# Linear attention with a feed-forward block on one core: batch 0's values in two loads, the first denominators in two single banks, and a new order for both

## The chip, the cores and the metric

The kernel runs on one core of a Trainium2 chip. The metric is the device time of one execution in microseconds (us). TensorE multiplies matrices, VectorE and ScalarE do elementwise work and empty PSUM (the banks that TensorE writes), GpSimd does a few small operations, and SyncE issues every load and store. In the rows of the profile these are PE (PEld is its weight load), DVE, ACT, POOL and SP.

## The reference

```
q_p, k_p = phi(q), phi(k)            # 4 batches, 4 heads, 1088 positions, 32 -> 64 features
kv  = sum over s of k_p[s,f] * v[s,d]
z   = sum over s of k_p[s,f]
att = (q_p @ kv) / (q_p @ z + 1e-6)  # phi(x)[i*8+j] = (S1 x)[i] * (S2 x)[j]
x   = att with the heads side by side        # 4352 tokens x 128
h   = relu(x @ w_in)                         # 128 -> 2048
out = (s * h*h + b) @ w_out                  # 2048 -> 128
```

## The kernel before

The 4352 tokens are cut into nine tiles, the first of 256 tokens and eight of 512. For each batch the kernel forms the key features and sums them with the values; for each tile it forms the query features, numerators and denominators, divides, and runs the feed-forward block over eight pairs of hidden blocks. From tile 1 on, every feed-forward product is split into three passes on high and low parts; tile 0 is multiplied in one float32 form.

The work is written as generators, and one string, `ORDER`, is the whole program order: each token advances the generator of that name by one step, and a step's instructions go to their engines in that order. A second table, `ON_DVE`, lists the steps that go to VectorE instead of ScalarE or GpSimd. Every engine takes its instructions strictly in the order in which they were written.

The names that matter here:

- `c` and `z` are filler products of 256 and 512 columns on TensorE, written to a spare bank.
- `Ls`, `Lk0`, `Lv0`, `Lq1`, `Lw6` and the like issue loads on SyncE: the projections, keys, values, queries of tile 1, weights. `Lw2i` and `Lw2i+1` are block i of `w_in` and `w_out`, loaded in pieces of 256 KB; blocks 0 and 1 are one piece each, blocks 2 to 4 two pieces each. The tiles are `raw` in the rows. Below, "w6's second piece" is the second load of `Lw6`.
- `s` unpacks the projections into `sk` and copies them twice into `srep`; `w0`, `w1`, ... unpack weights (an activation on ScalarE, a shift of the low words on either engine, a join on VectorE).
- `k0`, `e0`, `v0` are the key features, key sums and value sums of batch 0. `k0` works in three groups of three chunks: projections in a bank `psa`, a copy to `kab`, and their outer product `ph`, which `v0` then sums with the values. `e0` and `v0` end in two copies into `st`.
- `q0`, `q1` are the query features of tiles 0 and 1 (two tiles `hp`, copies `br`, products `pq`). `q2` and later go a longer way: a small product into `hp` (line 419), a copy `abq`, a store to DRAM and loads back that spread it, the last four into `br`.
- `d0` and `n0` are the denominators and numerators of tile 0, `n1` both of tile 1. `00` to `07` are the feed-forward pairs of tile 0, `10` to `17` those of tile 1.

PSUM is in three pools: `hp` (two tiles of two banks), `ops` (one bank) and `psa` (three single banks).

SyncE has eight completion counters that its transfers take in turn, so a transfer is issued only when the one eight places earlier has landed. When SyncE issues one after such a wait thus tells when the earlier one landed.

The constants (own heads, identity, scale and bias) lie behind the values of batch 0 in one array and arrive in the same load, into `vc_sb`.

Of the kernel before, what the change touches and what calls it, by code (L numbers as in the profile page):

```python
# [9 lines left out]
F32 = mybir.dt.float32  # L10
# [28 lines left out]
DIRECT = (0, 1)  # L39
FIRST_F32 = (0, 1, 2, 3, 4, 5, 6, 7)  # L40
ORDER = """
c z Ls c z Lk0 c Lk0 Lw0 Lw2 s Lv0 Lq1 Lw8 z s c z c s s z z s w0 w2 k0 z s c k0 Lw6 k0 k0 k0 Lw1 k0 k0 w0 k0 w0 Lw4
Lw6 q0 c q0 Lq2 k0 Lw4 q0 Lw3 Lw5 Lw5 Lw7 Lw7 e0 e0 q0 Lw8 Lk1 e0 v0 v0 q0 w2 Lk1 e0 v0 w2 v0 q1 q1 q1 q1 e0 e0 w1
v0 z w1 q1 d0 v0 n1 d0 n0 w6 w6 q2 d0 c w4 d0 d0 n0 n1 Lv1 w4 w4 w1 q2 w4 w3 00 00 00 01 w3 w0 03 01 01 w5 w6 q2 00
02 Lw9 03 w8 w3 n1 w3 n1 01 03 Lw9 02 w5 04 02 w7 q2 w5 w7 n1 Lk3 q2 w0 03 05 n1 05 Lk3 02 w8 Lq3 w1 05 Lq4 q1 n1 04
q2 n1 k1 w8 06 w6 w7 04 n1 w9 05 07 06 w3 04 k1 w4 06 k1 n1 w9 w9 k1 w9 07 13 k1 07 w1 Lv1 Lv3 w6 06 q2 w5 13 13 10
q2 07 q2 k1 k3 10 q3 10 q3 13 14 10 07 w2 q2 13 k1 k3 k1 12 w2 w5 14 q3 k1 10 15 w7 q2 07 12 Lv2 14 12 k1 q3 Lk2 k3
10 k3 12 Lv3 11 14 w8 k3 12 w7 n2 k3 15 12 14 w8 07 q3 w9 15 n2 n2 13 14 11 15 11 17 n2 n2 Lk2 15 n2 16 15 q3 q3 n2
n2 11 11 Lq6 17 q4 q3 k2 16 n2 n2 20 k3 16 11 16 17 q3 q4 25 16 q4 17 q3 k3 q4 q4 16 20 22 20 k2 17 17 25 25 20 25
17 20 22 17 24 20 q4 22 q3 k2 22 25 24 24 k3 q4 Lv2 23 22 n3 q4 Lq5 23 24 q6 n3 23 q6 22 n3 Lq8 n3 24 21 23 21 27 q6  # L50
21 n3 k2 q4 25 23 q6 21 n3 27 26 24 n3 23 k2 27 n3 21 k2 q6 27 q8 q6 n3 q6 q6 n3 26 q4 26 k2 21 q0 30 q8 q4 k2 k2 27
q6 26 33 q6 k3 30 k2 30 q8 26 q5 n4 q5 q8 33 32 n4 30 30 26 33 n4 27 n4 n4 33 n4 33 32 31 q6 32 34 n4 27 31 30 31 32
31 n6 32 Lq7 n4 31 q5 n6 35 q8 q8 n6 34 32 q5 n6 31 34 n6 n6 35 34 n6 35 q5 36 37 n6 n6 35 q8 34 n6 34 36 61 33 36
35 37 36 35 60 37 37 36 27 61 63 q5 36 37 q8 q5 37 q8 61 61 60 60 64 61 37 63 63 60 60 q8 64 n4 63 63 64 65 60 q5 62
q8 64 65 61 64 62 65 q7 n8 n4 63 62 67 q7 n8 65 65 n8 62 q5 n8 62 q7 n8 66 67 q5 67 64 66 67 q7 65 67 66 q5 66 40 n8
42 66 40 n8 40 42 62 41 42 n5 66 40 q7 n5 n5 67 40 n8 42 41 45 67 n5 q7 44 41 42 n5 q7 40 n5 n5 41 45 43 45 41 45 45
42 43 n5 45 44 43 44 43 47 46 41 44 43 47 47 44 67 43 q7 46 46 n8 n5 n5 47 46 47 51 51 54 q7 n8 51 44 46 50 54 54 q7
51 51 46 47 54 50 54 53 50 47 56 53 52 50 53 q7 50 n7 50 52 54 n7 52 53 47 55 53 51 52 55 n7 52 55 85 53 56 55 55 56
57 57 57 52 56 56 n7 n7 55 85 57 80 57 81 85 56 85 57 80 85 81 n7 80 81 80 57 80 83 83 81 84 80 85 86 81 83 83 83 81
84 84 82 84 86 84 86 n7 84 n7 n7 86 n7 87 82 82 83 57 86 87 71 87 72 87 82 82 72 87 72 71 86 72 70 72 71 82 70 74 71  # L60
87 71 70 70 76 70 74 87 70 37 73 76 76 74 76 71 72 74 76 73 75 74 77 73 76 73 73 75 87 75 73 77 75 77 74 75 75 77 77
77 77 77 77 77 77
"""
ON_DVE = frozenset("""
a4 a6 a7 e1 e2 e3 e4 e5 e6 e7 e8 k0 m2 m3 m4 m5 m6 m7 m8 o00 o03 o06 o10 o15 o20 o25 o30 o35 q40 q43 q44 q50
q52 q76 q80 q81 r22 r24 r33 r37 r50 r61 r63 r65 r66 r76 r77 r87 s0 sb t1 t2 u13 u16 u20 u24 u26 u32 u33 u34
u36 u41 u44 u45 u47 u51 u55 u56 u57 u60 u62 u63 u65 u70 u71 u72 u73 u77 u81 u82 u83 u86 w0h w0l w1h w1l w2h
w2l w3b w3h w3l w4b w4h w4l w5b w5l w6l w7l w8b w8l w9b w9h w9l x2 x3 x4 x5 x8 y0 y3
""".split())
NS = 32 * 2 + 2 * R  # L70
CS, CB, CT = 0, 1, 32
# [28 lines left out]
def attn_ffn_kernel(ctx: ExitStack, tc: tile.TileContext, qT, kq, vc, s80, w_in, w_out, outT):  # L100
    nc = tc.nc
# [288 lines left out]
    qfeat, xhl, x_first = {}, {}, []  # L390
# [55 lines left out]
    def moving(pq, rows, h, e0, e1):  # L446

        if len(pq.shape) == 3:
            return [(pq[rows, h, e0:e1], e0, e1)]
        if (e0, e1) == (0, 2 * QUARTER):  # L450
            return [(pq[rows, h], e0, e1)]
        cuts = [e0, QUARTER, e1] if e0 < QUARTER < e1 else [e0, e1]
        return [(pq[rows, h, a // QUARTER, a % QUARTER:a % QUARTER + e - a], a, e) for a, e in zip(cuts, cuts[1:])]

    def parts_of(t, out, y, pq, start):
        halves = tiles[t][2]
        for k in range(max(len(x) for x in halves)):
            for h in range(H):
                for r in range(2):
                    if k < len(halves[r]):  # L460
                        b, e0, e1 = halves[r][k]
                        rows = slice(64 * r, 64 * r + 64)
                        for x, a, e in moving(pq, rows, h, e0, e1):
                            nc.tensor.matmul(out[r][32 * h:32 * h + 32, a:e], st_t[b][rows, y, h // 2, h % 2], x,  # L464
                                             start=(a == 0 and start), stop=True, skip_group_check=True)

    def inverse(dt, C, kept):
        rc = p1.tile([P, 32], F32, name="rc")
        nc.vector.tensor_scalar(out=rc[:, :2 * C], in0=dt.rearrange("p (c y) -> p c y", y=32)[:, :, 0],
                                scalar1=EPS, scalar2=None, op0=ALU.add)  # L470
# [261 lines left out]
```

## Time and profile before

| what | value |
|---|---|
| three timed runs | 228.83, 230.77, 230.79 us |
| their median | 230.77 us |
| the profiled execution | 229.11 us |
| its span, first to last instruction | 227.3 us |
| TensorE busy | 222.1 us |
| VectorE busy | 188.9 us |
| ScalarE busy | 176.6 us |
| loads and stores | 22.08 MB |

The profiled execution lasts 1.8 us longer than its span; that part lies around the instructions. Times in the rows further down are counted from the start of the span. Instructions of one engine overlap in their pipeline, so the start of the next one often lies before the end of the last.

### The profile page before, as it was taken

Reading aid. Unit: us, or ns where it says so; the run is one execution under the profiler, and the core shown is the slowest. Engines: PE = TensorE matmul, PEld = TensorE weight load, DVE = VectorE, ACT = ScalarE, POOL = GpSimd, SP = SyncE. Lnnn points to the kernel's source line nnn. Section 1 sums busy time; section 2 is a strip of 40 time slices with the busy share of each in tenths; the row PEclk is TensorE's granted clock in tenths of the full one; section 3 lists DMA queues with packets and bytes.
Section 4 is the critical chain, followed back from the end, with each engine's and each line's share of the span. In section 5 each row is a group of like instructions: output and inputs, shape, how many; then the busy total and the mean of one; then the engine's idle time right before and its main releaser. Section 6 shows DMA issues by size and latency. Waiting matters only on the chain.

```text
span 227.3 us, 4622 instructions
## 1 busy us (share of the span) xinstructions
PE 222.1 (98%) x1840; PEld 176.8 (78%) x1840; DVE 188.9 (83%) x269; ACT 176.6 (78%) x211; POOL 4.6 (2%) x14
## 2 busy tenths in 40 slices
PE   8989999999999999999999999999999999999994
PEld 5658788787877787888887878888878888887883
DVE  1979889998799969999778979997976597968682
ACT  3489989998968959886875779669767969788671
POOL 1001220000000000000000000000000000000000
PEclk9999999999999999999999999999999999999999
DMA  6999583830157443054000321200100001001001
GB/s 190 375 369 375 191 250 108 267 114 3 46 174 195 138 146 92 27 176 128 0 0 13 92 61 46 72 0 0 46 3 1 0 37 55 0 3 46 0 0 46
DMA packets 12204, 22.08 MB, mean 97 GB/s; under 512 B 1304, under 2 KB 2840, under 8 KB 12184
## 3 DMA queue, kind: packets, MB, share of 16 engines
q1 hardware_dynamic: 12184, 21.80, 29.3%
q8 instruction: 14, 0.23, 0.4%
q14 instruction: 6, 0.05, 0.1%
HBM read 18.65 MB, written 3.15 MB: 96 GB/s over the span
## 4 chain that ended last, share of the span: by engine, by line
PE 93%; DMA 3%; SPq 1%; ACT 1%; DVE 1%; issue 0%
PE hp L571 42%; PE ops L571 42%; PE psa L464 4%; DMA vc_sb<-vc 3%; PE psa L253 2%; PE hp L419 1%; PE psa L352 1%; PE hp L402 0%; SPq L185 0%; SPq L158 0%; PE hp L464 0%; ACT ot L619 0%; DVE pq L410 0%; PE psa L274 0%; ACT br L121 0%
## 5 line engine op out<-in xcount | busy, mean ns | idle before, releaser
L565 DVE TENSOR_TENSOR ul<-u,uh 128x1024 fp32r<-128x1024 f32 x64 | 77.8, 1218 | 8.4 <-ACT uh L121 6.3
L133 ACT ACTIVATE u<-hp 128x1024 f32<-128x1024 f32 (+1 forms) x60 | 57.8, 965 | 20.6 <-PE hp L571 9.7
L142 ACT ACTIVATE u<-u 128x1024 f32<-128x1024 f32 (+1 forms) x64 | 64.1, 1006 | 4.9 <-DVE u L131 3.5
L571 PE MATMUL hp<-xh,wil 128*128 128x512 f32 x128 | 51.1, 399 | 0.0
L571 PE MATMUL ops<-uh,wol 128*128 128x512 f32 (+1 forms) x128 | 50.4, 394 | 0.0
L571 PE MATMUL hp<-xl,wih 128*128 128x512 f32 x128 | 49.9, 390 | 0.0
L571 PE MATMUL hp<-xh,wih 128*128 128x512 f32 x128 | 49.9, 390 | 0.0
L571 PE MATMUL ops<-uh,woh 128*128 128x512 f32 (+1 forms) x128 | 49.6, 388 | 0.0
L121 ACT CAST uh<-u 128x1024 fp32r<-128x1024 f32 x34 | 35.6, 1052 | 7.0 <-DVE u L140 3.4
L571 PE MATMUL ops<-ul,woh 128*128 128x512 f32 (+1 forms) x128 | 39.3, 388 | 0.0
L121 DVE CAST uh<-u 128x1024 fp32r<-128x1024 f32 x30 | 20.7, 688 | 11.0 <-ACT u L142 10.6
L571 PEld LDWEIGHTS ops<-uh,wol 128*128 128x128 f32 x128 | 24.0, 188 | 6.8 <-issue 1.6
L571 PEld LDWEIGHTS hp<-xh,wil 128*128 128x128 f32 x128 | 24.0, 188 | 6.2 <-ACT u L133 0.5
L571 PEld LDWEIGHTS hp<-xl,wih 128*128 128x128 f32 x128 | 24.0, 188 | 5.2
L571 PEld LDWEIGHTS ops<-ul,woh 128*128 128x128 f32 x128 | 24.0, 188 | 5.1
L571 PEld LDWEIGHTS ops<-uh,woh 128*128 128x128 f32 x128 | 24.0, 188 | 4.7
L571 PEld LDWEIGHTS hp<-xh,wih 128*128 128x128 f32 x128 | 24.1, 188 | 4.7
L131 DVE TENSOR_SCALAR u<-hp 128x1024 f32<-128x1024 f32 x12 | 14.7, 1224 | 1.9 <-PE hp L571 1.0
L136 DVE TENSOR_TENSOR ph<-kab 128x768 f32<-128x768 f32 (+2 forms) x9 | 10.8, 1214 | 0.1
L464 PE MATMUL psa<-pq,st 64*32 64x256 f32 (+2 forms) x336 | 10.2, 330 | 0.0
L140 DVE TENSOR_TENSOR u<-u 128x1024 f32<-128x1024 f32 x8 | 9.6, 1215 | 0.4 <-ACT u L133 0.3
L202 ACT ACTIVATE w<-raw 128x512 f32<-128x512 f32 (+1 forms) x10 | 5.9, 587 | 4.3 <-DMA raw<-w_in 4.2
(86 smaller groups left out, 172.6 us busy)
## 6 DMA issues: line engine op xcount, KB each, us to landing
pq<-qd SPq DMA_DIRECT2D x14, 256.0 KB
br<-qd SPq DMA_DIRECT2D x28, 128.0 KB
raw<-w_in SPq DMA_DIRECT2D x8, 256.0 KB
qt<-qT SPq DMA_DIRECT2D x8, 256.0 KB
raw<-w_out SPq DMA_DIRECT2D x8, 256.0 KB
outT<-ot SPq DMA_DIRECT2D x7, 256.0 KB
kt<-kq SPq DMA_DIRECT2D x3, 320.0 KB
vt<-vc SPq DMA_DIRECT2D x3, 320.0 KB
```

The source lines that it names most:

```text
L121: (nc.vector.tensor_copy if key in ON_DVE else nc.scalar.copy)(out=out, in_=in_)
L131: nc.vector.tensor_scalar(out=out, in0=in_, scalar1=0.0, scalar2=None, op0=ALU.max)
L133: nc.scalar.activation(out=out, in_=in_, func=AF.Relu)
L136: (nc.vector if key in ON_DVE else nc.gpsimd).tensor_tensor(out=out, in0=in0, in1=in1, op=op)
L140: nc.vector.tensor_tensor(out=out, in0=in_, in1=in_, op=ALU.mult)
L142: nc.scalar.activation(out=out, in_=in_, func=AF.Square)
L202: nc.scalar.activation(out=out, in_=f32(high), func=AF.Prelu, scale=2.0 ** -112, alpha=2.0 ** 32)
L253: nc.tensor.matmul(out[32 * q:32 * q + 32], w, x, start=(q not in begun), stop=last, skip_group_check=True)
L352: nc.tensor.matmul(views[e][32 * q:32 * q + 32], sp[64 * e:64 * e + 64], kt[64 * e:64 * e + 64, a:a + w32], start=True, stop=True, skip_gr ...
L464: nc.tensor.matmul(out[r][32 * h:32 * h + 32, a:e], st_t[b][rows, y, h // 2, h % 2], x, start=(a == 0 and start), stop=True, skip_group_ch ...
L565: nc.vector.tensor_tensor(out=ul[:, :, :N], in0=u[:, :, :N], in1=f32(uh[:, :, :N]), op=ALU.subtract)
L571: nc.tensor.matmul(out, w, x, start=(first and k == 0), stop=(last and k == len(terms) - 1))
```

## The change

The load of `vc_sb` (662 KB) becomes two: values of chunks 0 to 5 (384 KB), then values of chunks 6 to 8 with the constants (278 KB). The first denominators no longer use an `hp` tile, but two `psa` banks, and are transposed by two instructions in place of one. `ORDER` and `ON_DVE` are written anew for both. From `44 43 ... q7 46 46 n8 n5 n5 47 46 47 51` to the end the order string is the same; ahead of that the feed-forward pairs keep nearly their sequence.

```
-VPARTS = [(VW + NCST,)] + [(5 * H * D, 4 * H * D)] * 3
+VPARTS = [(6 * H * D, 3 * H * D + NCST)] + [(5 * H * D, 4 * H * D)] * 3
...
     def first_denominators():
         M = TILES[0] // 2
-        den = ps_h.tile([P, 2, 512], F32, name="hp")
-        parts_of(0, [den[:, r, :M] for r in range(2)], 1, qfeat[0], True)
+        den = [ps_a.tile([P, 512], F32, name="psa")[:, :M] for r in range(2)]
+        parts_of(0, den, 1, qfeat[0], True)
         yield
         dt = p1.tile([P, NMAX], F32, name="dt")
-        nc.vector.transpose(out=dt[:, :2 * M].rearrange("p (r m) -> p r m", r=2), in_=den[:, :, :M])
+        for r in range(2):
+            nc.vector.transpose(out=dt[:, r * M:(r + 1) * M], in_=den[r])
         yield
         yield from inverse(dt[:, :2 * M], M // 32, first)
...
-c z Ls c z Lk0 c Lk0 Lw0 Lw2 s Lv0 Lq1 Lw8 z s c z c s s z z s w0 w2 k0 z s c k0 Lw6 k0 k0 k0 Lw1 k0 k0 w0 k0 w0 Lw4
+c z c Ls Lk0 Lk0 z Lw2 c c s s z c Lw0 w2 c c c s c z s k0 z c k0 Lv0 Lv0 w2 Lq1 s k0 c k0 c w0 w0 Lw1 k0 k0 w0 Lw6
...
-a4 a6 a7 e1 e2 e3 e4 e5 e6 e7 e8 k0 m2 m3 m4 m5 m6 m7 m8 o00 o03 o06 o10 o15 o20 o25 o30 o35 q40 q43 q44 q50
+a7 e1 e2 e3 e4 e5 e6 e7 e8 k0 k1 k2 m2 m3 m4 m5 m6 m7 m8 o00 o03 o06 o10 o15 o20 o25 o30 o35 q43 q50 q52 q64
...
```

On TensorE, from the end of the query features of tile 1 to the first feed-forward product (lines 277 and 274 end `e0` and `v0`, lines 650 and 651 are filler, 464 is `d0`, `n0` and `n1`, 419 is `q2`), before:

```order
L277 MATMUL psa<-vc_sb,zm 128x4
L274 MATMUL psa<-vc_sb,kvs 128x128
L650 LDWEIGHTS const-bfloat16-1.0
L650 MATMUL ops<-const-bfloat16-1.0 128x512
L464 MATMUL hp<-pq,st_291 32x128 x8
L464 MATMUL psa<-pq,st_291 32x256 x16
L464 MATMUL hp<-pq,st_291 32x128 x8
L419 MATMUL hp<-qt,sq 32x128 x8
L650 LDWEIGHTS const-bfloat16-1.0
L650 MATMUL ops<-const-bfloat16-1.0 128x256
L571 MATMUL hp<-x,w_00_92 128x256 x2
```

The same place after the change:

```order
L277 MATMUL psa<-vc_sb,zm 128x4
L274 MATMUL psa<-vc_sb,kvs 128x128
L651 LDWEIGHTS const-bfloat16-1.0
L651 MATMUL ops<-const-bfloat16-1.0 128x256
L651 LDWEIGHTS const-bfloat16-1.0
L651 MATMUL ops<-const-bfloat16-1.0 128x256
L464 MATMUL psa<-pq,st_302 32x128 x8
L464 MATMUL hp<-pq,st_302 32x128 x8
L419 MATMUL hp<-qt,sq 32x128 x8
L464 MATMUL psa<-pq,st_302 32x256 x16
L651 LDWEIGHTS const-bfloat16-1.0
L651 MATMUL ops<-const-bfloat16-1.0 128x256
```

`n0` has moved from behind `n1` to directly behind `d0`, and `q2` from behind `n1` to ahead of it.

On ScalarE, from the unpacked projections to the copies into `st` (lines 202 and 127 unpack weights; `w_10` is `w2`, `w_00` is `w0`, `w_01` is `w1`), before:

```order
L202 ACTIVATE sk<-s_raw 128x80
L121 COPY srep<-sk 128x64
L202 ACTIVATE w_00_92<-raw_114 128x256
L202 ACTIVATE w_10_94<-raw_116 128x256
L127 ACTIVATE raw_114<-raw_114 128x256
L121 COPY kab_137<-psa 128x2x96
L121 COPY br<-hp 128x2x128 x2
L127 ACTIVATE raw_116<-raw_116 128x256
L121 COPY br<-hp 128x512 x2
L121 COPY st_291<-psa 128x128
L202 ACTIVATE w_01_93<-raw_156 128x256
```

The same place after the change:

```order
L202 ACTIVATE w_10_94<-raw_113 128x256
L121 COPY srep<-sk 128x64
L127 ACTIVATE raw_113<-raw_113 128x256
L121 COPY srep<-sk 128x64
L202 ACTIVATE w_00_92<-raw_122 128x256
L127 ACTIVATE raw_122<-raw_122 128x256
L121 COPY kab_132<-psa 128x2x96
L121 COPY br<-hp 128x2x128 x2
L202 ACTIVATE w_01_93<-raw_156 128x256
L121 CAST wih<-w_00_92 128x256
L127 ACTIVATE raw_156<-raw_156 128x256
L121 COPY br<-hp 128x512 x2
```

Both copies into `srep` now stand on ScalarE behind the unpacking of `w2` (VectorE made one of them before), and the unpacking of `w1`, a cast and a shift stand ahead of the copies `br` of tile 1 instead of behind them.

On SyncE, the loads from the values of batch 0 to `w4`'s second piece (buffer numbers kept; 123 is `w8`, 148 `w6`, 156 `w1`, 166 `w4`, 121 and 191 the queries of tiles 1 and 2), before:

```order
L158 DMA vc_sb_82<-vc 128x1324
L176 DMA qt_121<-qT 128x512
L185 DMA raw0_123<-w_in 128x512
L185 DMA raw0_148<-w_in 128x512
L185 DMA raw1_156<-w_out 128x512
L185 DMA raw0_166<-w_in 128x512
L185 DMA raw0_148<-w_in 128x512
L176 DMA qt_191<-qT 128x512
L185 DMA raw0_166<-w_in 128x512
```

The same place after (156 is `w1`, 161 `w6`, 163 `w4`, 166 `w8`, 144 and 168 the queries):

```order
L158 DMA vc_sb_82<-vc 128x768
L158 DMA vc_sb_82<-vc 128x556
L176 DMA qt_144<-qT 128x512
L185 DMA raw1_156<-w_out 128x512
L185 DMA raw0_161<-w_in 128x512
L185 DMA raw0_163<-w_in 128x512
L185 DMA raw0_166<-w_in 128x512
L176 DMA qt_168<-qT 128x512
L185 DMA raw0_161<-w_in 128x512
L185 DMA raw0_163<-w_in 128x512
```

`w1` has moved from the fourth place behind the values to the second, and the queries of tile 2 from the seventh to the sixth.

## Rows read from the trace of the kernel before

**Rows 1.** The page: busy time, share of the span and instructions of each engine.
```profile
PE 222.1 (98%) x1840; PEld 176.8 (78%) x1840; DVE 188.9 (83%) x269; ACT 176.6 (78%) x211; POOL 4.6 (2%) x14
```

**Rows 2.** Windows: stretch, busy time by engine with instructions, granted clock, transfers' share, GB/s.
```profile
15.80:223.30 207.50, 207.50 (x1565) 167.08 (x1565) 179.17 (x245) 168.33 (x192) 3.34 (x6) 1.00 0.26 82
```

**Rows 3.** The chain that ended last, in order of time: start, length, what.
```profile
3.07 6.17 DMA vc_sb<-vc
...
15.29 0.30 PE hp L419 x16
...
15.80 2.95 PE hp L571 x12
...
19.62 0.86 PE hp L571 x4
...
68.23 1.02 PE psa L464 x32
```

**Rows 4.** TensorE's timeline: start, length, what; in brackets idle time before it.
```profile
9.37 1.21 PE L253 MATMUL psa<-ph,vc_sb 128*32 128x64 f32 x72 [0.49 <-DMA vc_sb<-vc]
10.51 1.12 PE L402 MATMUL hp<-qt,srep 32*64 32x256 f32 x32
...
13.12 0.45 PE L464 MATMUL hp<-pq,st 64*32 64x128 f32 x16 [0.64 <-DVE pq L410]
```

**Rows 5.** VectorE's timeline, 8 to 22 us.
```profile
8.70 0.95 DVE L136 TENSOR_TENSOR ph<-kab 128x768 f32<-128x768 f32 x1
...
12.29 1.29 DVE L410 TENSOR_TENSOR pq<-hp,br 128x512 f32<-128x512 f32 x2 [0.77 <-ACT br L121]
13.67 0.45 DVE L485 STREAM_TRANSPOSE dt<-hp 128x256 f32<-128x256 f32 x1
...
14.60 0.45 DVE L475 STREAM_TRANSPOSE rr<-rc 128x256 f32<-128x256 f32 x1
15.33 0.42 DVE L495 TENSOR_TENSOR x<-hp,rr 128x256 f32<-128x256 f32 x1 [0.28 <-PE hp L464]
...
21.34 0.70 DVE L475 STREAM_TRANSPOSE rr<-rc 128x512 f32<-128x512 f32 x1
```

**Rows 6.** ScalarE's timeline, 2 to 17 us.
```profile
2.65 0.27 ACT L202 ACTIVATE sk<-s_raw 128x80 f32<-128x80 f32 x1 [0.63 <-DMA s_raw<-s]
...
6.83 0.44 ACT L202 ACTIVATE w<-raw 128x256 f32<-128x256 f32 x1 [3.34 <-DMA raw<-w_in]
7.47 0.44 ACT L202 ACTIVATE w<-raw 128x256 f32<-128x256 f32 x1 [0.21 <-DMA raw<-w_in]
7.81 0.44 ACT L127 ACTIVATE raw<-raw 128x256 int32<-128x256 uint32 x1
8.15 0.30 ACT L121 COPY kab<-psa 128x192 f32<-128x192 f32 x1
8.40 0.65 ACT L121 COPY br<-hp 128x256 f32<-128x256 f32 x2
...
11.67 1.07 ACT L121 COPY br<-hp 128x512 f32<-128x512 f32 x2 [2.29 <-PE hp L402]
12.63 0.28 ACT L121 COPY st<-psa 128x128 f32<-128x128 f32 x1
...
14.42 0.70 ACT L202 ACTIVATE w<-raw 128x512 f32<-128x512 f32 x1 [0.68 <-DMA raw<-w_in]
...
16.97 0.60 ACT L133 ACTIVATE u<-hp 128x512 f32<-128x512 f32 x1
```

**Rows 7.** SyncE's timeline: the first load, and two issues that waited for earlier ones.
```profile
0.74 0.39 SPq L152 DMA_DIRECT2D s_raw<-s  x1
...
14.35 0.33 SPq L185 DMA_DIRECT2D raw<-w_in  x1
15.02 0.33 SPq L158 DMA_DIRECT2D kt<-kq  x1
```

**Rows 8.** VectorE's timeline at tile 2's features: the product behind the last load of `br`.
```profile
38.67 1.22 DVE L136 TENSOR_TENSOR pq<-pq,br 128x1024 f32<-128x1024 f32 x1
```

More of the change, by code (lines that the diff above doesn't have):

```diff
@@ L41 @@
 ORDER = """
-c z Ls c z Lk0 c Lk0 Lw0 Lw2 s Lv0 Lq1 Lw8 z s c z c s s z z s w0 w2 k0 z s c k0 Lw6 k0 k0 k0 Lw1 k0 k0 w0 k0 w0 Lw4
[L43 to L61, printed above, removed]
@@ L62 @@
-77 77 77 77 77 77
+c z c Ls Lk0 Lk0 z Lw2 c c s s z c Lw0 w2 c c c s c z s k0 z c k0 Lv0 Lv0 w2 Lq1 s k0 c k0 c w0 w0 Lw1 k0 k0 w0 Lw6
+Lw4 z Lw8 Lq2 k0 k0 q0 k0 q0 Lw6 q0 q0 Lw4 Lw3 Lw5 w1 q0 w0 v0 e0 e0 e0 v0 v0 Lw5 q1 v0 c w1 c Lw7 Lw7 Lw8 e0 e0 w2
+v0 Lk1 c q1 c q1 q1 q1 e0 v0 d0 d0 d0 n0 s w6 d0 q2 n1 q2 c d0 n0 w4 w4 w3 w4 00 Lk1 w3 w1 01 00 w6 00 Lw9 n1 w4 01
+03 w5 w6 w3 00 02 01 n1 03 w5 01 w5 03 Lw9 w0 q2 q2 n1 w7 04 02 w7 w8 n1 n1 n1 03 w7 Lv3 05 k1 w8 w4 02 w8 w7 02 05
+n1 k1 n1 Lv1 Lv3 q2 05 05 w3 06 Lk3 w9 04 Lv1 q2 Lk3 07 q2 04 Lq3 w1 w9 n1 04 06 13 w9 k1 06 06 w9 07 w1 Lq4 q2 w6
@@ new lines @@
+07 w5 Lk2 07 13 10 13 w6 k1 k1 10 q2 k1 q3 k3 w2 13 13 w2 07 10 Lv2 w5 14 q2 q3 10 07 k1 k1 k3 12 w8 10 14 Lq5 12 k3
+12 k1 Lq8 w8 q2 10 13 Lk2 k3 k1 12 q3 k3 14 14 11 q3 q3 n2 k3 12 11 n2 w7 15 11 14 n2 w3 11 q3 12 q3 15 14 15 q3 n2
+17 15 k3 n2 11 n2 17 15 16 n2 n2 15 q4 k2 n2 17 Lq6 q3 16 n2 17 q4 16 17 20 16 20 20 11 k3 q4 k2 w9 16 25 q3 16 20
+q3 25 25 22 20 k2 17 k3 22 q4 Lv2 25 22 24 23 k2 k2 25 17 24 24 q4 k3 20 22 22 q4 24 n3 24 23 q6 Lq7 n3 23 k2 24 k2
+q6 n3 n3 23 n3 21 q6 n3 q6 k2 26 21 n3 q6 n3 22 q4 21 23 n3 q4 26 q6 q6 21 q6 25 21 27 26 k2 26 27 27 n3 q6 26 30 30
@@ new lines @@
+33 q4 q4 q0 23 q6 21 k2 q4 27 26 n4 27 q8 n4 30 n4 n4 33 q5 27 q5 q8 q6 30 33 17 32 31 30 n4 33 n4 27 30 q8 q8 33 32
+34 32 31 n4 31 n6 32 n4 35 32 q8 34 q5 33 34 31 n6 q8 n6 31 35 34 q8 n6 34 36 32 q5 q8 n6 37 q5 q5 n6 q8 35 36 n6 n6
+36 n6 35 31 35 q1 36 n6 36 34 q5 37 61 37 36 63 61 61 q5 q8 37 q8 37 q5 61 63 61 60 63 35 60 37 63 63 65 60 64 60 07
+37 60 65 64 65 60 64 n8 q7 65 62 63 65 q7 q5 n4 64 62 n4 66 n8 64 62 61 n8 62 n8 66 62 n8 40 65 67 66 66 66 67 q5 62
+66 67 n8 n8 67 41 40 67 40 40 42 40 42 41 42 q7 n8 n5 64 67 42 45 n5 n5 n5 42 27 67 n5 41 43 40 45 44 q7 n5 41 42 n5
@@ new lines @@
+45 41 45 n5 45 43 45 44 43 47 46 44 44 43 43 q7 41 q7 q7 47 44 47 67 43 q7 46 46 n8 n5 n5 47 46 47 51 51 54 q7 n8 51
+44 46 50 54 54 q7 51 51 46 47 54 50 54 53 50 47 56 53 52 50 53 q7 50 n7 50 52 54 n7 52 53 47 55 53 51 52 55 n7 52 55
+85 53 56 55 55 56 57 57 57 52 56 56 n7 n7 55 85 57 80 57 81 85 56 85 57 80 85 81 n7 80 81 80 57 80 83 83 81 84 80 85
+86 81 83 83 83 81 84 84 82 84 86 84 86 n7 84 n7 n7 86 n7 87 82 82 83 57 86 87 71 87 72 87 82 82 72 87 72 71 86 72 70
+72 71 82 70 74 71 87 71 70 70 76 70 74 87 70 37 73 76 76 74 76 71 72 74 76 73 75 74 77 73 76 73 73 75 87 75 73 77 75
@@ L63 @@
+77 74 75 75 77 77 77 77 77 77 77 77
 """
 ON_DVE = frozenset("""
-a4 a6 a7 e1 e2 e3 e4 e5 e6 e7 e8 k0 m2 m3 m4 m5 m6 m7 m8 o00 o03 o06 o10 o15 o20 o25 o30 o35 q40 q43 q44 q50
-q52 q76 q80 q81 r22 r24 r33 r37 r50 r61 r63 r65 r66 r76 r77 r87 s0 sb t1 t2 u13 u16 u20 u24 u26 u32 u33 u34
-u36 u41 u44 u45 u47 u51 u55 u56 u57 u60 u62 u63 u65 u70 u71 u72 u73 u77 u81 u82 u83 u86 w0h w0l w1h w1l w2h
-w2l w3b w3h w3l w4b w4h w4l w5b w5l w6l w7l w8b w8l w9b w9h w9l x2 x3 x4 x5 x8 y0 y3
+a7 e1 e2 e3 e4 e5 e6 e7 e8 k0 k1 k2 m2 m3 m4 m5 m6 m7 m8 o00 o03 o06 o10 o15 o20 o25 o30 o35 q43 q50 q52 q64
@@ L69 @@
+q76 q80 q81 r26 r30 r41 r50 r66 r76 r77 r87 sb t1z t2z t3 u11 u13 u17 u21 u22 u24 u30 u31 u32 u33 u34 u35 u37
+u40 u41 u43 u47 u51 u55 u56 u57 u60 u61 u63 u65 u67 u70 u71 u72 u73 u77 u81 u82 u83 u86 w0l w1h w1l w2h w2l
+w3h w3l w4b w4h w4l w5b w5l w6b w6h w6l w7h w7l w8b w8l w9h w9l x1 x2 x5 x8 y0 y3
 """.split())
```

## The prediction

> **What bounds the kernel now.** I read the busy times first [rows 1]: TensorE is busy 222.1 of 227.3 us. The windows say where the rest lies [rows 2]: from 15.8 to 223.3 us TensorE is busy 207.50 of 207.50 us, at a granted clock of 1.00, the upper of its two levels (2.4 GHz). No wait is left there to remove, and the change issues the same products; it could only tear a new hole. So what the change can give lies ahead of 15.80, where the first feed-forward product starts [rows 3]. All the work moved ahead of that product is the same before and after: `k0`, `q0`, `e0`, `v0`, `q1`, `d0`, `n0`, `n1`, `q2`. I therefore price the change by one number, the start of that product, and then ask whether the later work keeps pace with it.
>
> Ahead of 15.80 TensorE idles twice: 0.49 us until the values land, and 0.64 us until 13.12, where the first denominators wait [rows 4]. Around these it runs fillers.
>
> **The split load.** The load of 662 KB lands at about 9.3 [rows 3, 4]. The queue is full, so its halves land by bytes: 384 of 662 KB of the 1.8 us since 7.47, when the weight piece ahead of it landed [rows 6], gives 8.5, and the second load still ends at 9.3. Two thirds of the value sums (1.21 us in all) can thus run ahead of 9.37. But the last third waits for the third product `ph` on VectorE, 8.70 to 9.65 [rows 5], which the split doesn't touch; here it moves. Both `srep` copies now stand on ScalarE behind `w2`, whose load lands at 6.83. From there in order: `w2` 6.83, copy 7.17, shift 7.3, copy 7.65, `w0` 7.8, shift 8.15, the copy `kab` 8.45 (it stood at 8.15), `br` 8.7 (8.40). The step of 0.34 for 256 columns is 7.47 to 7.81, and of a short copy I take less than the 0.25 between 8.15 and 8.40 [rows 6]. VectorE's third product then runs 8.9 to 9.85 instead of 8.70 to 9.65, and what follows on VectorE by the same 0.2.
>
> TensorE: keys done at 8.0, `q0` 8.0 to 8.7, a third of the values 8.7, key sums, another third to 9.7, the last third 9.9 to 10.35 where it ended at 10.58; `q1` then 10.35 to 11.4 where it ended at 11.63 [rows 4]. So the split is worth 0.2 us here. It isn't passed on. ScalarE now unpacks `w1` and does two more steps ahead of the copies `br` of tile 1. `w1`'s load is the second behind the values: at 0.65 to 0.85 us a piece (0.65 is 14.35 to 15.02 [rows 7]; 0.85 is 9.3 to 14.35, six pieces) it lands at 10.6 to 11.0. Three steps of 0.34 later the copies start at 11.65 to 12.0, where they started at 11.67 [rows 6].
>
> The Trainium skill ("DMA: Bandwidth & Descriptors", Rules for kernel authors and Anatomy of one DMA) speaks against the split: it advises coalescing into large transfers, and gives a fixed cost of about 2.0 us for each. The trace differs while transfers queue: neighbours land 0.65 us apart [rows 7], with no such gap between them. By the Trainium skill's figure the second half would land at about 11.3, which is rival 4 below.
>
> **The two banks.** In `hp`, `d0` waited for the first product `pq` of tile 1, which ends near 12.94 (half of 12.29 to 13.58 [rows 5]). Without it `d0` still waits for the copy into `st`, which ended at 12.63 + 0.28 = 12.91 [rows 6]. So the bank alone frees 0.03 us, and I book it at nothing. The copy stands two `br` copies (0.96 us) behind their start: 12.6 to 12.95 now, and `d0` starts at 13.1 to 13.45, where it was 13.12. Its two transposes cost more than one: 256 columns take 0.45 us and 512 take 0.70 [rows 5], so 0.2 is fixed, and half of it or a little more is paid again: 0.15. In return `n0` stands directly behind `d0`, which removes VectorE's 0.28 us of waiting ahead of `x` [rows 5]. `x` started at 15.33; the sum is 15.33 - 0.28 + 0.15 + (0 to 0.35) = 15.2 to 15.55, it takes 0.42, so VectorE lets the first product start at 15.65 to 16.05 against 15.80.
>
> **The order of q2.** This is the term that I expect to decide. `q2` now stands ahead of `n1`. It needs the queries of tile 2, whose load was the seventh piece behind the values and landed just ahead of 15.02; the sixth, `w6`'s second piece, landed just ahead of 14.35, as both SyncE's next issue and ScalarE's wait to 14.42 show [rows 6, 7]. After the change the queries are the sixth. TensorE arrives at `q2` at about 13.7 (`d0` at 13.1, then 16 + 16 products like `d0`'s), waits to 14.4, does `q2` (0.3 to 0.4 [rows 3]), then `n1` (32 products, 1.02 [rows 3]) and a filler of 0.1: the first product starts at 14.4 + 0.35 + 1.02 + 0.1 = 15.9. Ends for the landing: six pieces at 0.65 from 9.3 is 13.2, and then VectorE's 15.65 decides; its old place, 15.02, gives 16.5. I take 14.35, since the sixth piece of the same size landed there. **First product: 15.9, which is +0.1; ends -0.15 and +0.7.**
>
> **After the start.** ScalarE reaches the first relu behind `w6`, whose second piece lands one place later (+0.65), without `w6`'s shift (512 columns, moved to VectorE, -0.70) and with `w3`'s (256 columns, +0.34): 16.97 [rows 6] becomes 17.25. The third pair of products waits for that relu's bank and may lose up to 0.2 more than the start. But before, twelve products took 2.95 us where later four take 0.86 [rows 3], so over 0.3 was lost there already, part of it to `abq`, which `q2`'s earlier place now removes. I book nothing, with ends of -0.2 and +0.2. From `w4`'s second piece on the loads stand in the same places as before. The feed-forward pairs keep their neighbours, and VectorE (188.9) and ScalarE (176.6) keep 38 and 50 us of idle time [rows 1], so a reshuffled `ON_DVE` moves work within slack: nothing, with the exception named as a rival.
>
> **The sum.** 0.1 + 0 + 0. On the profiled execution (229.11, span 227.3) that is 229.2; on the median of 230.77 it is 230.9. The three runs spread over 0.85%, 228.83 to 230.79, so 1% is about what a measurement of this kernel can tell from no change.
>
> **The rivals.**
> 1. Faster: tile 2's queries land before 14.0, `w1`'s load before 10.3, so that ScalarE starts the `br` copies when `q1` ends, at about 11.25. Then all of `d0` moves ahead by 0.4, and VectorE's 15.65 becomes 15.25. Against it stands that the sixth piece landed at 14.35; for it, that six pieces at the later pace of 0.65 would land by 13.2. Price -0.15 to -0.55: 230.2 to 230.6.
> 2. Slower: the queries land no earlier than they did, 15.02, since SyncE still issues them behind a load that waits for `w0`'s join, now 0.2 later. It decides once they land after 14.2 (13.7 plus the 0.5 by which TensorE would then be ahead of VectorE's 15.65), and every 0.1 beyond costs 0.1. Price +0.7: 231.5.
> 3. Slower: the last load of `br` for tile 2 now stands on SyncE behind a load of values that waits for `k1`'s value sums, near 35 us. If it lands after 38.67 [rows 8], VectorE stops in front of the product, with all later splits queued behind it, and TensorE misses them some 2 to 3 us later. At 35 plus about 1 us of issues and its bytes it should be in time. Price: 1 us for each us past about 41; at 2 us, 232.9.
> 4. Slower: the second half pays a load's own latency in full. The 80 KB of the projections took from 0.74 to 2.65, 1.9 us, into an empty queue [rows 6, 7]; with that on top the constants come at 11.2, the last third of the values ends at 11.6, `q1` at 12.7, the `st` copy starts at 13.7, `d0` at 14.2, and the first product 1.0 later: 231.8. Against it stand the 0.65 us between neighbours. The fixed cost of the Trainium skill's page would act as this does.
> 5. The split does nothing at all, because the last third never was late for it: -0.2 of `q1` is lost, which ScalarE hides anyway. The time is that of the forecast.
>
> **How the numbers follow.** Forecast with rival 5: 0.6. Rival 1: 0.22. Rival 2: 0.12. Rival 3: 0.04. Rival 4: 0.02. The range takes the lower of the runs with rival 1 at its best, 228.83 - 0.4 = 228.4, and the upper with rivals 2 and 4, 230.79 + 1.0 = 231.8; what lies outside is rival 3 and the odd median. Faster by over 1% needs under 228.46, so rival 1 and a median at the lower runs: 0.06. Slower by over 1% needs 233.1, rival 3 at its worst: 0.03. Within 1%: 0.91.
>
> **What would show it.** Right: the values' first third on TensorE starts near 8.7, ahead of the key sums, and the last third near 9.9 with VectorE's `ph` as what it waited for; the `br` copies of tile 1 start at 11.65 or later; TensorE waits ahead of line 419 for a load to about 14.4; the first line 572 product starts between 15.65 and 16.1; from there to the last product 207.5 us, give or take 0.4. Wrong: a first product ahead of 15.5 or behind 16.3, TensorE idle time after 16 us, or a load of values that lands well behind 9.5.

## The result, and the profile after

The changed kernel takes 232.05 us (median of 13 executions, 230.77 to 232.59); the kernel before, beside it, 229.95 (13 executions, 228.83 to 232.04). The ratio is 1.0079, with a 95% interval of 1.0053 to 1.0105: 1.2 to 2.4 us slower, 1.8 in the middle. The forecast was +0.1, and 232.05 lies above the 231.8 at which the range of the working ended, though within the 1% that had the chance of 0.91. The ratios here and below leave out executions more than 1.5% above the fastest of their kernel, the medians do not. The profiled execution of the changed kernel is its shortest, 230.77 us with a span of 228.8, so its trace shows 1.5 of the 1.8 us.

Lines past 486 of the changed kernel carry numbers one higher: its 566 and 572 are 565 and 571 of before. First the page, as [rows 1], then windows, as [rows 2].

```profile
PE 222.3 (97%) x1847; PEld 177.4 (78%) x1847; DVE 186.5 (82%) x269; ACT 176.9 (77%) x212; POOL 3.7 (2%) x14
```

```profile
15.94:80.00 64.06, 63.95 (x708) 50.80 (x707) 58.73 (x103) 56.37 (x77) 2.09 (x6) 1.00 0.52 163
80.00:90.00 10.00, 9.03 (x114) 6.96 (x112) 6.47 (x10) 5.11 (x6) 0.00 (x0) 1.00 0.39 124
90.00:223.44 133.44, 133.44 (x739) 107.98 (x740) 110.83 (x134) 107.36 (x110) 0.00 (x0) 1.00 0.13 40
```

TensorE, which before had no gap from the first feed-forward product on, now loses 0.97 us between 80 and 90 us (and 0.11 ahead of 18), and VectorE and ScalarE do 2 us less there than in the same stretch of before, which follows.

```profile
80.00:90.00 10.00, 10.00 (x155) 7.87 (x143) 8.52 (x15) 6.97 (x12) 0.00 (x0) 1.00 0.35 109
```

The start came out as forecast. TensorE's timeline after, to be read beside [rows 4]:

```profile
8.70 0.54 PE L253 MATMUL psa<-ph,vc_sb 128*32 128x64 f32 x24
...
10.12 0.54 PE L253 MATMUL psa<-ph,vc_sb 128*32 128x64 f32 x24 [0.40 <-DVE ph L136]
10.59 1.28 PE L402 MATMUL hp<-qt,srep 32*64 32x256 f32 x32
...
13.05 0.45 PE L464 MATMUL psa<-pq,st 64*32 64x128 f32 x16 [0.18 <-ACT st L121]
...
14.57 0.45 PE L419 MATMUL hp<-qt,sq 64*32 64x128 f32 x16 [0.66 <-DVE rc L472]
...
15.94 3.14 PE L572 MATMUL hp<-x,w 128*128 128x256 f32 x12
18.91 1.03 PE L572 MATMUL ops<-u,w 128*128 128x258 f32 x4
```

The first product of line 572 starts at 15.94, where 15.9 was forecast. The last row is the first product into `ops`, behind the third pair; it is read further down beside that of before:

```profile
18.59 1.03 PE L571 MATMUL ops<-u,w 128*128 128x258 f32 x4
```

What went wrong is 70 us further on. VectorE's timeline of the changed kernel, and then that of before, at tile 4's features:

```profile
86.07 1.23 DVE L136 TENSOR_TENSOR pq<-pq,br 128x1024 f32<-128x1024 f32 x1 [3.00 <-DMA br<-qd]
87.22 1.22 DVE L566 TENSOR_TENSOR ul<-u,uh 128x1024 fp32r<-128x1024 f32 x1
```

```profile
82.00 1.23 DVE L136 TENSOR_TENSOR pq<-pq,br 128x1024 f32<-128x1024 f32 x1 [0.60 <-DMA br<-qd]
83.14 1.22 DVE L565 TENSOR_TENSOR ul<-u,uh 128x1024 fp32r<-128x1024 f32 x1
```

VectorE stands 3.00 us in front of the product, for tile 4's last `br` load, and the split `ul` stands behind it. TensorE's two idle times are these, one in front of the products that read `pq`, one in front of the products whose bank a late relu frees:

```profile
87.35 1.12 PE L464 MATMUL psa<-pq,st 64*32 64x256 f32 x43 [0.30 <-DVE pq L136]
...
89.54 0.45 PE L419 MATMUL hp<-qt,sq 64*32 64x128 f32 x16 [0.67 <-ACT u L133]
```

The chain of the changed kernel ties them together, in order of time:

```profile
81.01 0.57 SPq L439
81.58 0.04 issue
81.63 4.43 DMA br<-qd
...
86.07 0.06 DVE pq L136
...
87.22 1.23 DVE ul L566
...
88.47 1.03 ACT u L133
...
89.54 0.45 PE hp L419 x16
```

Why that load leaves so late is in SyncE's issues, after and then before (tile 6 is the next tile whose features go through DRAM):

```profile
61.37 1.19 SPq L435 DMA_DIRECT2D pq<-qd  x2
...
72.22 1.59 SPq L428 DMA_DIRECT2D qd<-abq  x2
76.03 0.58 SPq L435 DMA_DIRECT2D pq<-qd  x1
76.65 1.25 SPq L439 DMA_DIRECT2D br<-qd  x2
77.95 0.54 SPq L435 DMA_DIRECT2D pq<-qd  x1
78.54 3.66 SPq L439 DMA_DIRECT2D br<-qd  x6
```

```profile
65.50 0.62 SPq L439 DMA_DIRECT2D br<-qd  x1
...
66.64 0.60 SPq L439 DMA_DIRECT2D br<-qd  x1
...
70.75 0.59 SPq L439 DMA_DIRECT2D br<-qd  x1
...
74.81 1.19 SPq L435 DMA_DIRECT2D pq<-qd  x2
76.05 3.07 SPq L439 DMA_DIRECT2D br<-qd  x5
```

In both, tile 4's `pq` loads leave by 65.5. Before, three of its `br` loads left by 71.3 and only the fourth stood behind tile 6's `pq` loads, as the third of the five at 76.05. After, all four stand behind tile 6's first `pq` load at 76.03, which waits 2.1 us for tile 6's store to land, and they go out mixed with tile 6's own: the two at 76.65, and the fourth and fifth of the six at 78.54. The new `ORDER` differs here too, far from the edit at the start.

### The profile page after: what moved, and what is told of

Its sections match the earlier page's. It is cut to its first block, busy times and chain, and to the rows that moved or that the text cites. A ratio compares the mean times of both kernels' runs of the same rounds, so it can differ in the third digit from the quotient of the medians.

```text
span 228.8 us, 4635 instructions
## 1 busy us (share of the span) xinstructions
PE 222.3 (97%) x1847; PEld 177.4 (78%) x1847; DVE 186.5 (82%) x269; ACT 176.9 (77%) x212; POOL 3.7 (2%) x14
## 4 chain that ended last, share of the span: by engine, by line
PE 75%; DMA 8%; DVE 6%; ACT 4%; SPq 4%; issue 2%; DVEq 0%; ACTq 0%
PE ops L572 35%; PE hp L572 35%; DMA raw<-w_in 4%; DVE ul L566 3%; PE psa L464 3%; SPq L439 2%; DMA br<-qd 2%; DMA vt<-vc 1%; PE psa L253 1%; ACT u L133 1%; ACT w L202 1%; ACT u L142 1%; PE hp L419 1%; DVE ph L136 1%; PE psa L352 0%
## 5 line engine op out<-in xcount | busy, mean ns | idle before, releaser
L133 ACT ACTIVATE u<-hp 128x1024 f32<-128x1024 f32 (+1 forms) x64 | 62.0, 970 | 20.6 <-DVE ul L566 9.9
L142 ACT ACTIVATE u<-u 128x1024 f32<-128x1024 f32 (+1 forms) x65 | 65.5, 1008 | 3.9 <-DVE u L131 2.3
L121 ACT CAST uh<-u 128x1024 fp32r<-128x1024 f32 x29 | 30.4, 1052 | 10.7 <-PE ops L572 6.9
L121 DVE CAST uh<-u 128x1024 fp32r<-128x1024 f32 x35 | 24.1, 688 | 10.2 <-ACT u L142 6.7
L136 DVE TENSOR_TENSOR pq<-pq,br 128x1024 f32<-128x1024 f32 x7 | 8.6, 1223 | 5.2 <-DMA br<-qd 3.0
L131 DVE TENSOR_SCALAR u<-hp 128x1024 f32<-128x1024 f32 x8 | 9.8, 1224 | 0.9 <-PE hp L572 0.2
```

Source lines behind the costliest of these rows:

```text
L121: (nc.vector.tensor_copy if key in ON_DVE else nc.scalar.copy)(out=out, in_=in_)
L131: nc.vector.tensor_scalar(out=out, in0=in_, scalar1=0.0, scalar2=None, op0=ALU.max)
L133: nc.scalar.activation(out=out, in_=in_, func=AF.Relu)
L136: (nc.vector if key in ON_DVE else nc.gpsimd).tensor_tensor(out=out, in0=in0, in1=in1, op=op)
L142: nc.scalar.activation(out=out, in_=in_, func=AF.Square)
```

## The experiments

All ratios are to the kernel before, run on the same chip in the same series; there are three such series, on three chips. The changed kernel was not run again in them, so a run is set against it by way of the two ratios, or trace against trace. The names in the order text are those of the loops: `q4` is a step of tile 4's features; its seventh to tenth steps issue the four `br` loads (the fifth and sixth the two `pq` loads).

**Tile 4's br loads early**, in the changed kernel; nothing else is moved. The four tokens go from their places among `q6` to behind the second `pq` load:

```diff
-20 22 22 q4 24 n3 24 23
+20 22 22 q4 q4 q4 q4 q4 24 n3 24 23
...
-n3 22 q4 21 23 n3 q4 26
+n3 22 21 23 n3 26
...
-30 30 33 q4 q4 q0 23
+30 30 33 q0 23
```

> The changed kernel with one thing moved: tile 4's four br loads stand right behind its own two pq loads on SyncE, ahead of everything of tile 6. Theory Q (the loss is SyncE's order at tile 4: its br loads stood behind tile 6's pq load, which waits for tile 6's store): VectorE's 3.00 us wait in front of tile 4's pq product goes, TensorE's idle 0.30 and 0.67 us at 87.35 and 89.54 go, and the kernel is 0.8 to 1.3 us faster than the changed one; the first feed-forward product still starts at 15.94. Theory S (the loss is made in the first 20 us, by the split load, the two banks or the order there, and the wait near 85 us only takes up time that would be lost later anyway): within 0.3 us of the changed kernel.

Measured: 229.59 us (12 executions, 229.04 to 230.52), ratio 0.9994 (0.9966 to 1.0022). Against the changed kernel's 1.0079 the loss is gone, some 2 us, more than the 0.8 to 1.3 expected; between the two traces the last product comes 1.12 earlier. VectorE's timeline has the product without a wait, and TensorE is busy 10.00 of the 10 us from 80 to 90. The first product starts at 15.87, 0.07 earlier than in the changed kernel, so the loss went without the start being touched. Theory S falls.

```profile
83.04 1.21 DVE L136 TENSOR_TENSOR pq<-pq,br 128x1024 f32<-128x1024 f32 x1
```

**The late order put into the kernel before.** SyncE's loads of tiles 4 and 6 get the order that the changed kernel has; nothing else moves.

```diff
-24 24 k3 q4 Lv2 23 22 n3 q4 Lq5
+24 24 k3 Lv2 23 22 n3 Lq5
...
-k2 q4 25 23 q6 21
+k2 25 23 q6 21
...
-n3 21 k2 q6 27 q8 q6 n3 q6 q6 n3 26 q4 26
+n3 21 k2 q6 q4 q4 27 q8 q6 n3 q6 q6 q6 q4 q4 n3 26 26
...
-k2 k2 27 q6 26 33
+k2 k2 27 26 33
```

> The kernel before, with SyncE's loads of tiles 4 and 6 put into the order that they have in the changed kernel: all four br loads of tile 4 behind tile 6's first pq load. Nothing else changes. Theory Q: the pq load of tile 6 leaves at 74.8 as before, the last br load of tile 4 some 5.6 us behind it and lands 4 to 5 us later, so tile 4's product moves from 82.0 to 84 to 85.5; TensorE, which wants that product at 85.89, idles there or at the next relu, and the kernel is 0.3 to 1.0 us slower than before. Theory S: nothing over 0.2 us.

Measured: 235.67 us (6 executions, 232.09 to 237.11); the ratio, which rests on three of them, is 1.0172 (1.0098 to 1.0246). All six lie above the longest of 29 executions of the kernel before, 231.64. The direction is theory Q's, the size is larger than the 0.3 to 1.0 that I expected: the shortest is already 2.3 above the median of before. The mean granted clock was 1.000 in the shortest, 0.993 in two and 0.985 in the three longest. There is a trace of the longest alone (237.11 us), and its numbers hold for that one; VectorE's timeline, TensorE's, and two windows of it:

```profile
87.78 1.23 DVE L136 TENSOR_TENSOR pq<-pq,br 128x1024 f32<-128x1024 f32 x1 [5.00 <-DMA br<-qd]
```

```profile
91.31 0.68 PE L419 MATMUL hp<-qt,sq 64*32 64x128 f32 x16 [4.25 <-ACT u L133]
```

```profile
90.00:92.00 2.00, 0.69 (x27) 0.69 (x35) 2.00 (x4) 1.77 (x3) 0.00 (x0) 0.50 0.00 0
...
96.00:98.00 2.00, 2.00 (x8) 1.55 (x8) 0.50 (x3) 1.15 (x2) 0.00 (x0) 0.84 0.60 181
```

The last load left by 80.8, as expected, and landed 6.9 us later, not 4 to 5. In this kernel's order little of the wait is hidden, 0.75 us: 5.00 us on VectorE become 4.25 us of TensorE idle. Behind it the granted clock is 0.50, the lower level (1.2 GHz), until about 96.6 (0.84 is the mean of 0.64 us at 0.50 and 1.36 at 1.00). The sum: its last product starts 8.0 us later than before; 1.3 of that it had already at 69 us, which the edit has no part in, 4.25 is the idle time, and the 2.4 left fit the five microseconds at half clock.

**The split alone**, in the kernel before: the two sizes of the changed kernel and one more `Lv0` behind the first.

```diff
-VPARTS = [(VW + NCST,)] + [(5 * H * D, 4 * H * D)] * 3
+VPARTS = [(6 * H * D, 3 * H * D + NCST)] + [(5 * H * D, 4 * H * D)] * 3
...
-Lw2 s Lv0 Lq1
+Lw2 s Lv0 Lv0 Lq1
```

> The kernel before with the split load alone: batch 0's values and constants in two loads, one right behind the other, everything else as it was. Theory Q: the first value sums start up to 0.7 us earlier, but what ends last there (ScalarE's copies of br and st) does not move by more than 0.2 us; start of the first feed-forward product 15.6 to 16.0, time within 0.3 us of before. Theory S with the split as its cause: the start is 0.3 us or more later, and the time 0.5 to 2 us longer.

Measured: 231.03 us (12 executions), ratio 1.0021 (0.9989 to 1.0053); first product at 15.79. All value sums ran from 9.37 to 10.58 before; now the last third runs at 9.53, behind `ph`, `q1` starts at 10.01 instead of 10.51, the `br` copies at 11.17 instead of 11.67 and `d0` at 12.62 instead of 13.12. The first product does not follow: line 419 waits 0.40 us for tile 2's queries, to 15.28. Nor is the 0.5 clearly the split's, since `q1` starts between 10.09 and 10.71 in three other traces of kernels with one load.

```profile
15.28 0.45 PE L419 MATMUL hp<-qt,sq 64*32 64x128 f32 x16 [0.40 <-DMA qt<-qT]
```

**One load again**, in the changed kernel: the same edit of `VPARTS` backwards (the second `Lv0` then does nothing).

> The changed kernel with batch 0's values and constants in one load again, everything else as changed. Theory Q: the last third of the value sums moves by 0.2 to 0.5 us and the start of the first feed-forward product by 0 to 0.3; the wait in front of tile 4's product and the idle time behind it stay, and the time is within 0.3 us of the changed kernel. Theory S with the split as its cause: the time falls back to that of the kernel before, by 1.5 us or more.

Measured: 231.97 us (12 executions), ratio 1.0074 (1.0042 to 1.0107), that of the changed kernel. First product at 16.17, 0.23 later, behind a pause of 0.91 us in tile 0's numerators that the last section describes, so not by the load; `q1` starts at 10.61, where the changed kernel has 10.59. Neither edit of the split shows it to be worth anything, at the first product or in the time. This run, the profiled execution at 232.58, also shows what a longer wait costs; VectorE's timeline and the windows:

```profile
87.92 1.23 DVE L136 TENSOR_TENSOR pq<-pq,br 128x1024 f32<-128x1024 f32 x1 [4.51 <-DMA br<-qd]
```

```profile
80.00:90.00 10.00, 8.20 (x75) 6.59 (x79) 5.25 (x7) 4.41 (x6) 0.00 (x0) 1.00 0.51 133
90.00:100.00 10.00, 9.33 (x146) 7.25 (x136) 9.66 (x16) 7.97 (x10) 0.00 (x0) 1.00 0.24 77
```

TensorE loses 1.80 + 0.67 = 2.47 us to a wait of 4.51; the changed kernel lost 0.97 to one of 3.00. Both times 2.0 us of the wait are hidden, and the rest is paid one for one. By that, an estimate, a wait near 4 us would give the median of the changed kernel; I have no trace of such an execution, so about half a microsecond of the 1.8 stays unseen.

**The four br loads in one row, still behind tile 6's first pq load**, in the changed kernel:

```diff
-n3 q6 n3 22 q4 21 23 n3 q4 26
+n3 q6 q4 q4 q4 q4 n3 22 21 23 n3 26
...
-30 30 33 q4 q4 q0 23
+30 30 33 q0 23
```

> The changed kernel with tile 4's four br loads still behind tile 6's first pq load and its wait, but in one row, ahead of tile 6's second pq load and br loads. Theory Q1 (it is the place behind the load that waits which costs): they leave at 76.6 to 78.6 and at the 4.4 us that the last one took to land in the changed kernel tile 4's product could start at about 83.1, when VectorE comes to it in the kernel with the early loads: most of the loss goes, the time is within 0.4 us of that kernel. Theory Q2 (eight br and two pq loads of 128 and 256 KB go in one burst at some 140 GB/s, and what costs is that tile 4's last ones share it with tile 6's): the same direction if those ahead of it count alone, since only one pq load stands ahead, but with all ten sharing the engines the product starts at 84.5 or later and half of the loss or more stays (0.6 us and up above that kernel).

Measured: 229.43 us (12 executions, 229.00 to 229.89), ratio 0.9958 (0.9936 to 0.9979). SyncE's timeline, then VectorE's:

```profile
75.96 0.58 SPq L435 DMA_DIRECT2D pq<-qd  x1
76.58 2.50 SPq L439 DMA_DIRECT2D br<-qd  x4
```

```profile
83.40 1.23 DVE L136 TENSOR_TENSOR pq<-pq,br 128x1024 f32<-128x1024 f32 x1 [0.39 <-DMA br<-qd]
```

This corrects my theory. Standing behind the load that waits costs a wait of 0.39 us, out of the 2.0 that are hidden. What costs is the place in the row behind it: SyncE gives out one load each 0.62 us, so with four of tile 6's loads in between tile 4's last one leaves 2.5 us later (81.6 against 79.1), and the product starts 2.67 later. From the end of its issue it lands in 4.3 us here and 4.4 in the changed kernel; in the two runs with the longer waits it took 6.1 and 6.9 with the same loads ahead. So sharing the transfer engines, theory Q2, is at most an addition that differs by execution; why it differs isn't shown.

**The two banks alone**, in the kernel before, with `n1` behind `n0` (a third bank of the pool is free at once, a second one only behind the transposes):

```diff
-q1 d0 v0 n1 d0 n0 w6 w6 q2
+q1 d0 v0 d0 n0 n1 w6 w6 q2
```

> The kernel before with tile 0's denominators in two banks of the small PSUM pool, and tile 1's n products behind tile 0's (its second bank is free only behind the two short transposes). Theory Q: tile 0's numerators follow its denominators at once, x is ready at about 15.5 as before, tile 1's products end near 15.2 and tile 2's L419 products, behind them, near 15.65, so the first feed-forward product starts at 15.6 to 15.85; time within 0.3 us of before. Theory S with the banks as its cause: the start is later by 0.3 us or more and the time by 0.5 to 2.

Measured: 230.10 us (12 executions), ratio 0.9979 (0.9950 to 1.0008). No change in the time, though in the profiled execution the first product starts at 17.02, far from the 15.6 to 15.85 expected: tile 0's numerators waited 0.36 us for the second copy into `st`, which I had not counted, and the last of them came behind a pause of 1.09 us that the last section describes and doesn't explain. Neither half of the edit costs time by itself.

**An earlier start**, three kernels, all with tile 4's `br` loads early. In the first tile 2's products of line 419 go behind tile 1's. In the second, on ScalarE, `w1`'s shift also goes behind the `st` copies and `w3`'s unpacking behind the first relu (the last change of the diff). The third is the second without that last change.

```diff
-d0 q2 n1 q2
+d0 n1 q2 q2
...
-c w1 c Lw7
+c c Lw7
...
-e0 v0 d0 d0
+e0 v0 w1 d0 d0
...
-w4 w3 w4 00 Lk1 w3 w1 01 00 w6
+w4 w4 00 Lk1 w1 01 00 w3 w3 w6
```

> The kernel with tile 4's br loads early, and in addition tile 2's L419 products behind tile 1's products on TensorE. If the wait for tile 2's queries (they land near 14.4) is what the start of the changed kernel was late by: tile 1's products start when the second transpose ends, near 14.05 instead of 14.71, L419 follows near 15.15, and the first feed-forward product starts at 15.55 to 15.7 instead of 15.87; time 0.1 to 0.3 us shorter than with the early loads alone. If something else (x, at 15.44 there) sets it: no change.

> As the kernel with tile 2's L419 products behind tile 1's, and two things more on ScalarE: the 0.43 us conversion of the second weight part that stood ahead of tile 1's br copies goes behind the st copies, and the unpacking of the fourth part, 0.7 us, behind the first relu. br copies 0.25 us earlier, st copies, denominators, x too; the first feed-forward product starts at 15.3 to 15.5, the first relu 1.1 us later; the third pair may wait for its weights, which land near 15.8 and are joined near 17.4. Time 0.3 to 0.6 us shorter than with the early loads alone if nothing waits, none if the third pair's weights take over as the bound.

> As the kernel with the earlier start, but the unpacking of the fourth weight part stays ahead of the first relu. First feed-forward product at 15.3 to 15.5, first relu near 17.0 instead of 16.6, ops products near 18.6; time within 0.3 us of that kernel and 0.4 to 1.2 us shorter than before.

Measured, in that order: 229.70, 229.49 and 229.59 us; ratios 0.9960 (0.9932 to 0.9987), 0.9948 (0.9919 to 0.9976), 0.9972 (0.9945 to 0.9999). The first product starts at 15.55, 15.41 and 15.33, as expected, up to 0.54 us ahead of 15.87. The end follows in the first alone: the last product starts at 223.69, 223.85 and 224.17, against 223.95 with the `br` loads early alone and 223.63 before, so of 0.32, 0.46 and 0.54 us at the start 0.26, 0.10 and nothing arrive. In the third, TensorE waits 0.58 us in front of the third pair for a relu, while VectorE waits for a weight load to 15.92; in the second it waits 0.29 us at 67.13. So most of what is gained at the start is given back.

These three and the kernel with the `br` loads in one row beat the kernel before in their series, by 0.3 to 0.5%. The kernel with the `br` loads early, whose trace is like theirs, did not beat the kernel before in its own series, so a gain over before is not settled. What differs between the series is the kernel before: its medians are 229.75, 230.80 and 229.78 us, while the five kernels lie between 229.43 and 229.70 in all three.

**Tile 4's last two br loads early in the kernel before**, so that it has no wait there either:

```diff
-22 n3 q4 Lq5
+22 n3 q4 q4 q4 Lq5
...
-k2 q4 25 23
+k2 25 23
...
-n3 26 q4 26
+n3 26 26
```

> The kernel before with the last two br loads of tile 4 right behind its first two, so that none stands behind tile 6's pq load. VectorE's wait of 0.60 us in front of tile 4's product at 82.00 goes (0.69 and 0.81 in two variants of that kernel). If the spread of the kernel before (228.8 to 231.9) comes from this wait growing past what TensorE can bear in some executions, the median falls by 0.4 to 1.2 us and the spread shrinks to about 1 us, as in the variants of the changed kernel with the loads in one row. If the spread comes from elsewhere (the pause of 0.3 to 1.4 us that TensorE shows near 14 us), no change.

Measured: 230.43 us (12 executions, 229.43 to 233.05), ratio 1.0051 (1.0020 to 1.0081). The wait of 0.60 us went and nothing was gained, which fits its being inside the slack. That it is 0.5% slower I can't explain: its trace, of its shortest execution, has no idle TensorE time behind a first product at 16.24. The median did not fall as it would have if the spread of the kernel before came from this wait, so that isn't its source.

## Why the prediction was wrong where it was

**The steps up to the first product held, in part by luck.** The first third of the values ran at 8.70 (forecast 8.7) and the last third waited for `ph`, at 10.12 (9.9). `q1` started at 10.59, where 10.35 was forecast; in the two kernels with only the `br` loads moved, the same program up to there, it started at 10.14 and 10.10. As forecast it didn't matter: the `br` copies started at 11.75 (11.65 to 12.0), and at 11.67 and 11.63 in those two. `d0` waited for the `st` copy, to 13.05 (13.1 to 13.45). The two transposes took 0.51 us against 0.45, so the second cost 0.06, not 0.15; `x` started at 15.13 (15.2 to 15.55). Line 419 waited to 14.57 (14.4). Its row puts that down to VectorE's `rc`; but in the kernel with the `br` loads in one row it started at 14.32, ahead of the end of `rc` at 14.40, and the row names the queries, as the prediction does:

```profile
14.32 0.45 PE L419 MATMUL hp<-qt,sq 64*32 64x128 f32 x16 [0.64 <-DMA qt<-qT]
```

The first product started at 15.94 (15.9). That it fits within 0.04 is luck: it started at 15.87 and 15.69 in those two kernels, and at 15.80, 16.42 and 16.24 in three kernels that share the program of before up to there. A shift of 0.1 can't be told from that spread.

**Pricing the change by that one number failed.** From there to the start of the last product before took 207.8 us, the changed kernel 209.1, and the three kernels with earlier starts 208.1 to 208.8. The prediction's own sign of being right was 207.5 give or take 0.4, and idle time of TensorE behind 16 us was one of its signs of being wrong. A start moved by 0.5 us is not a time moved by 0.5 us: in the kernel with one load again the first product came 0.23 later than in the changed one, and the `ops` products behind the third pair at 18.86, 0.05 earlier.

**The step that failed** is the one after the start: "I book nothing, with ends of -0.2 and +0.2". It measured +1.3 in the profiled execution: 1.12 behind 19 us, by tile 4's loads (with those loads early 0.05 of it is left), and 0.18 by the third pair, whose `ops` products began at 18.91, 0.32 later than before, of which the start is 0.14. The reason given was false: "From `w4`'s second piece on the loads stand in the same places as before." In the order string that holds up to the second `Lk1`; behind it the sequence of loads and stores differs almost up to the end, and tile 4's four `br` loads are what costs. The first relu came at 17.31 (17.25 forecast) and cost the third pair the "up to 0.2" that I named and then did not book.

**Rival 3 had the mechanism and the wrong tile.** A `br` load behind a load that waits, VectorE stopped in front of the product, splits behind it, TensorE short some microseconds later: all of that happened, but at tile 4. Tile 2's last load left at 35.7, and its product ran at 40.23 without a wait. The rival looks at SyncE's order for tile 2 alone, and had a chance of 0.04. Its price, one for one past some 2.3 us, was nearly right: 2.0 us of the wait are hidden in the changed kernel's order, 0.75 in the one trace of the late order in the kernel before.

**The other rivals.** Rival 1 (start earlier) and rival 2 (queries at 15.02) did not happen. Rival 4 is excluded by the split alone, in which the last third waited for `ph` and not for its load, as it did in the changed kernel itself. The fixed cost of about 2.0 us that the Trainium skill ("DMA: Bandwidth & Descriptors", Anatomy of one DMA) gives, fitted there on transfers that GpSimd issues, isn't seen between queued neighbours here: two landed 0.67 us apart (15.02 less 14.35, which the prediction puts at 0.65). Rival 5 is near the truth for the split. The reason for expecting nothing behind 16 us was that TensorE had no gap and VectorE and ScalarE had 38 and 50 us to spare. Spare time of an engine in the whole span says nothing of a product that it has to start by about 85 us (83.07, where the wait began, and the 2.0 that are hidden).

## What to carry to other kernels

When a change brings a new program order, compare the whole order of the queue that issues the transfers, not only the edited part: for each load, what waits ahead of it and how many loads go out between that and itself, at 0.62 us each here, against the time at which its consumer's slack ends. Loads that belong to one consumer go out in one row, ahead of the next consumer's. And an engine that is never idle is no proof that a change can cost nothing there: such an engine can only lose, so look for the wait of another engine that is nearest to reaching it.

## What the runs showed that I had not expected

TensorE pauses near 14 us in nine of these twelve kernels with nothing that the profile shows to wait for, and the pause differs. The weight loads of the kernel before, of the one with the late order and of the one with its last two `br` loads early (the same program up to there), and of the two banks alone:

```profile
14.05 0.32 PEld L464 LDWEIGHTS psa<-pq,st 64*32 64x32 f32 x16 [0.27 <-issue]
```

```profile
14.67 0.32 PEld L464 LDWEIGHTS psa<-pq,st 64*32 64x32 f32 x16 [1.31 <-issue]
```

```profile
14.48 0.32 PEld L464 LDWEIGHTS psa<-pq,st 64*32 64x32 f32 x16 [0.85 <-issue]
```

```profile
15.51 0.10 PEld L464 LDWEIGHTS hp<-pq,st 64*32 64x32 f32 x1 [1.36 <-issue]
```

In one and the same program it differs from 0.27 to 1.31 us, and with it the time from `d0` to the first product: 2.68, 3.71 and 3.26 us in the first three. The 1.03 between them is more than the 0.85 that the prediction's range for this start spans. In all nine kernels the pause has the same place in TensorE's stream, behind 221 or 222 products, at times from 13.57 to 15.51 and in front of different products. So it goes with that place and not with what is computed there; what TensorE waits for stays open. The other surprise is the price of an idle TensorE: 4.25 us without work were followed by some 5 us at a granted clock of 0.50, where idle times of 2.47 us (in two pieces) and 0.97 were not; each is one trace.
